# Tokens-on-partitions attention, a softmax minimum as bias, DMA turns, and gate products on GpSimd

## The chip, the cores and the metric

The kernel runs on one core of a Trainium2 chip. The metric is the device time of one execution in microseconds. Beside the times there is a profile of one execution: for every instruction its engine, start, duration, tiles and source line, and for every DMA its packets. PE is the tensor engine (its weight loads are shown as PEld), DVE the vector engine, ACT the scalar engine, POOL is GpSimd, SP the engine that issues most DMAs of this kernel.

## The reference

Linformer attention, then a gated feed-forward network. There are 8 batches and 8 heads, 1024 tokens and 64 columns a head; keys and values are projected from 1024 tokens to 64.

```python
k_proj = einsum('ks,bhsd->bhkd', E, k)
v_proj = einsum('ks,bhsd->bhkd', F, v)
scores = q @ k_proj^T / sqrt(64)
scores = scores - max(scores, axis=-1)
attn   = exp(scores) / (sum(exp(scores)) + 1e-9)
x      = (attn @ v_proj), heads side by side      # 8192 x 512
gate   = sigmoid(x @ w_gate)                      # 512 x 1536
val    = x @ w_val
out    = (gate * val) @ w_out                     # 8192 x 512, float32
```

## The kernel before

**Tiling.** Everything on PE is bf16 with float32 sums in eight PSUM banks (`pF0..3`, `pA0..3`). A batch is two blocks of 512 tokens; 1024 tokens of a head are held as 128 partitions x 8 rows, and two tokens' 64-column head rows share one 128-column piece (`g` = 0, 1 says which of the two). The feed-forward work of a block is done with Strassen-like seven-product schemes (`seven`, `o_jobs`): a product is four (or twelve) matmuls of 256 columns, ACT copies a bank to another bank or to SBUF in between (`copyG`, `snapG`, `copyO`, ...), DVE adds banks to SBUF buffers (`plus`). A *quad* K is one third of a block's gate and value work, so a batch has six quads and two output blocks. `quad_jobs` makes for a quad four gate tiles (`tanh` on ACT, since the sigmoid is taken as (1 + tanh(x/2))/2) and four gate products into `hT` (`hidden`, L1276). In two of the four, the value is still in PSUM; in the other two both gate and value lie in SBUF, in the spare buffers. `s_sum` forms sums of `hT` on DVE for the output products, and `xs_sum` forms sums of `xT` for the quads.

**Attention of a batch b >= 1.** POOL issues the loads of K, V and Q as one DMA each (`load_kv`, `load_q`), which turn float32 to bf16. `kv` projects K and V (L503 matmuls of 128x64 weights and 512 columns), `keep_kd` and `keep_vd` take the result out with ACT, `turn_kd` turns K by a DMA transpose on SP (L1526), and `transpose_q` turns Q in four (L1449). `sc_one` makes the scores with the 64 projected keys on partitions and tokens in the free dimension, four matmuls of 64x64 weights side by side; `h_exp` takes the exponential of a whole 128x512 bank in one ACT instruction, without the maximum. `den8` sums over keys with PE, `rec` takes reciprocals on DVE, `gather` (8 small DMAs) and `spread` (POOL `partition_broadcast`, L1618, into the K/V tiles) lay them out, `xo_one` multiplies by the values, and `mul` (L1649, DVE) scales the result into `xT`. In batch 1 the reciprocals are spread by PE matmuls and ACT copies instead (`out_jobs_pe`, with `bck`). Batch 0 has its own code (`h_*`).

**Order.** Each piece of work is a `job` on an engine with a position `pos`, counted in quads. `Scheduler.run` simulates the engines when the kernel is built, with costs given with every operation, and takes on each engine the ready job of lowest position, as long as it is within a `window` of PE's earliest open job and the banks and buffers that it needs are free. The order that comes out is the program of each engine; on the chip the engines run their lists strictly in order and wait on semaphores. `Plan.add` finds these waits from the keys that an operation reads (`r`), writes (`w`) or holds (`x`, the PSUM bank):

```python
            if o.eng == eng and o.dma is None:
                if eng == "PE":
                    return
            deps[id(o)] = o
```

So only PE is excused from waiting on its own engine. The same keys tie a bank's users together.

Of the kernel before, what the change touches and what calls it, by code (L numbers as in the profile page):

```python
# [6 lines left out]
AF = mybir.ActivationFunctionType  # L7
# [13 lines left out]
NI = DM // P  # L21

# [111 lines left out]
class Scheduler:  # L134
# [64 lines left out]
    def safe(self, group, got):  # L199
        left = {k: len(f) for k, f in self.free.items()}  # L200
        for g, _ in got:
            left[g.kind] -= 1
        taken = [g for g, _ in got]
        todo = []
        for g in self.groups + ([] if any(group is x for x in self.groups) else [group]):
            need, held = {"bank": 0, "buf": 0}, {"bank": 0, "buf": 0}
            for x in g:
                if x.at is None and not any(x is y for y in taken):
                    need[x.kind] += 1
                elif x.left:  # L210
                    held[x.kind] += 1
            todo.append((need, held))
# [11 lines left out]
    def take(self, j, t):  # L224
# [30 lines left out]
        return True  # L255

# [28 lines left out]
    def run(self):  # L285
# [17 lines left out]
        while left:  # L303
            moved = True
            while moved:
# [4 lines left out]
                for e in engines:  # L310
# [3 lines left out]
                    for item in sorted(self.open[e], key=lambda i: (i[0], i[1])):  # L314
                        if item[0] > limit:
                            break
# [17 lines left out]
def bass_linformer_attn__then__ffn_glu_sigmoid_kernel(  # L334
# [20 lines left out]
    with contextlib.ExitStack() as es:  # L355
# [9 lines left out]
        def within(shape, dtype):  # L365
# [21 lines left out]
        xS = [sbuf(f"xS{i}", [P, 4, 2, 256], BF16) for i in range(2)]  # L387
        early[0], used[0] = xS[0][:, :, :, :].rearrange("p a b c -> p (a b c)"), 0
# [3 lines left out]
        rhl = within([P, 256], BF16)  # L392
        quad = sbuf("quad", [P, 1], FP32)
# [12 lines left out]
        rb = (  # L406
            KVs[:, :, :, :].rearrange("p w h c -> p (w h c)").bitcast(FP32)
            .rearrange("p (n c) -> p n c", n=8)
        )
        rrow = (  # L410
            Qb[:, :, :].rearrange("p h c -> p (h c)").bitcast(FP32)
            .rearrange("p (i c) -> p i c", i=4)
        )
        kpd = sbuf("kpd", [64, H, 2, DH], BF16)
        kpD = sbuf("kpD", [P, H, DH], BF16)
        vpD = [sbuf(f"vpD{i}", [P, H, DH], BF16) for i in range(2)]
        qT = sbuf("qT", [P, H, 512], BF16)
        eT = sbuf("eT", [P, 8, 512], BF16)
        rden = sbuf("rden", [P, 256], FP32)
        xT = [sbuf(f"xT{i}", [P, NI, 2, 512], BF16) for i in range(2)]  # L420

# [6 lines left out]
        NB = 11  # L428
# [10 lines left out]
        sched = Scheduler(range(8), range(2 + NB), 20.6, 1.3, 38.8)  # L439
# [53 lines left out]
        def mm(b, o, lhsT, rhs, r, start=True, stop=True, tp=None, tr=False, read=False, n=512, conc=1, fill=0.0):  # L493
# [5 lines left out]
            else:  # L499
# [4 lines left out]
                r=r,  # L504
                x=[bk_(b)],
# [34 lines left out]
        def turned():  # L540
            return [("qT", r) for r in range(NR)]

        def load_kv(n, src, b, after=()):
            load(
                KV[n][:, :, :],
                src[b].rearrange("h (p t) d -> p h (t d)", t=NT),
                [("KV", n, 0), ("KV", n, 1)] + [("rb", 4 * n + x) for x in range(4)],
                f"KV{n}",
                r=list(after),
                nbytes=MB2,  # L550
            )
# [10 lines left out]
        def load_q(b):  # L562
            load(
                Qb[:, :, :],
                q[b].rearrange("h (p t) d -> p h (t d)", t=NT),
                [("Q", hf, R) for hf in range(2) for R in range(2)]
                + [("rrow", i, x) for i in range(4) for x in range(2)],
                "Q",
                nbytes=MB2,
            )  # L570
# [189 lines left out]
        def v_part(R):  # L760
# [14 lines left out]
            vv = vpD[0][:, :, :].rearrange("p (r h) d -> p r h d", h=2)  # L775
            for n, (h, g) in enumerate(((0, 0), (1, 1), (0, 1), (1, 0))):
                o = vv[64 * g : 64 * g + 64, pairs(R), h, :]
                i = bank[bks[h]][64 * h : 64 * h + 64, 0:128].rearrange("p (r d) -> p r d", d=DH)
                ws = [("vpD", 0, h, g, R)]
# [5 lines left out]
        def turn_k(R):  # L785
            bk = whole.next()
            ob = bank[bk][:, :].bitcast(BF16)
            for n, r in enumerate((2 * R, 2 * R + 1)):
# [11 lines left out]
                kpD[:, 4 * R : 4 * R + 4, :].rearrange("p h c -> p (h c)"),  # L800
                ob[:, 0:256],
                [],
                [("kpD", R)],
# [3 lines left out]
        def VPD(s, R):  # L807
            return [("vpD", s, h, g, R) for h in range(2) for g in range(2)]
# [28 lines left out]
        def h_sc(hf, R, bks):  # L837
            for rr in range(2):
                for c in range(2):
                    h = 4 * R + 2 * rr + c  # L840
                    for g in range(2):
# [4 lines left out]
                            kpD[gg, h, :],  # L846
                            qT[gg, h, 256 * hf : 256 * hf + 256],
                            [("kpD", R), ("qTh", hf, R, rr)],
# [9 lines left out]
        def h_den(Rs, bk):  # L858
            for n in [2 * R + g for R in Rs for g in range(2)]:
                for c in range(4):  # L860
# [5 lines left out]
                        [("dsel8", n % 2), ("eT", n)],  # L866
# [51 lines left out]
        def h_xo(R, bks):  # L918
            for rr in range(2):
                for g in range(2):  # L920
                    for c in range(2):
# [5 lines left out]
                            vpD[0][kk, h, :],  # L927
                            eT[kk, 2 * R + g, 256 * rr : 256 * rr + 256],
                            VPD(0, R) + [("eT", 2 * R + g)],
# [9 lines left out]
        def h_scale(hf, n, bk):  # L939
            R, g = n // 2, n % 2  # L940
            o = xT[0][:, 2 * R : 2 * R + 2, hf, 256 * g : 256 * g + 256]
# [12 lines left out]
        def h_scale_part(hf, n, j, bk):  # L954
# [4 lines left out]
                    xT[0][:, 2 * R + j, hf, 256 * g : 256 * g + 256],  # L959
# [119 lines left out]
        def mm_one(blk, m, i, n, pb):  # L1079
# [5 lines left out]
                xT[s][:, i, hf, :],  # L1085
                [("w" + n, m // 2, i // 2), ("xT", s, i, hf, 0), ("xT", s, i, hf, 1)],
# [45 lines left out]
        def x_part(blk, n):  # L1132
            s, hf = blk // 2 % 2, blk % 2
            if n[0] == "S":
# [3 lines left out]
                xT[s][:, i0 : i0 + 2, hf, 256 * tok : 256 * tok + 256],  # L1138
                [("xT", s, i0 + i, hf, tok) for i in range(2)],
            )  # L1140

        def xs_sum(blk, n):
# [7 lines left out]
            if blk == 2:  # L1150
                w = w + ["bsel8", ("kp", 0), ("kp", 1)]
                w += [(k, R) for k in ("rhi", "rhl") for R in range(2)]
# [99 lines left out]
        def quad_jobs(K, pos):  # L1252
# [4 lines left out]
            def gate(half_, tok, b, s, p):  # L1257
# [6 lines left out]
                job("ACT", p + 0.01, body, name="tanh")  # L1264

            def value(half_, tok, b, s, p):
# [4 lines left out]
                def body():  # L1271
# [3 lines left out]
                    dve(  # L1275
                        lambda e: e.scalar_tensor_tensor(  # L1276
                            o,
                            y.rearrange("p (j c) -> p j c", j=2),
                            1.0,
                            x.rearrange("p (j c) -> p j c", j=2),  # L1280
# [91 lines left out]
        def o_jobs(blk, pos, step, last=False):  # L1372
# [52 lines left out]
            for n in (1, 2, 3):  # L1425
                s_jobs(n, min(pos, ready + 0.1 * n))
# [431 lines left out]
```

## Time and profile before

| | us |
|---|---|
| three runs | 536.17, 536.48, 533.93 |
| median | 536.17 |
| the profiled execution, its own time | 535.25 |
| its span in the profile | 533.5 |

The span runs from the first to the last recorded instruction; the execution's own time has some microseconds around it. Per engine the page gives busy time, number of instructions and, for each group, the mean duration and the idle time before it with what ended it. The 40 slices cut the span into pieces of 13.3 us. Busy durations overlap at the ends where an engine starts one instruction before the one before has ended, so starts are also read from the timeline.

| group | count | mean ns |
|---|---|---|
| matmul, 128x128 weights, 256 columns, any product | most of 4757 | 273 |
| ACT 128x512 from PSUM to a spare buffer | 266 | 598 |
| DVE gate product, both inputs in SBUF (`hT<-spare`) | 76 | 736 |
| DVE gate product, value in PSUM | 36 and 33 | 675 and 678 |
| POOL `PARTITION_BROADCAST` | 96 | 892 |
| DMA transpose of Q, issue to landing | 24 | 3300 |

### The profile page before, as it was taken

What the parts mean: (1) busy time and instruction counts of PE and PEld (TensorE: products, weight loads), DVE (VectorE), ACT (ScalarE), POOL (GpSimd) and SP (SyncE); (2) the same over time, 40 slices, a digit from 0 to 9 for tenths busy, and PEclk for the clock granted to TensorE, in tenths of its full rate; (3) what the DMA queues carried; (4) which work ended last, traced back from release to release, by engine and by line L of the source; (5) the groups of instructions that cost most, each with busy time, mean ns of one, the idle gap of its engine ahead of it and who ended that gap; (6) DMA issues with size and microseconds to landing.
All of it is one profiled execution on the core that took longest, in us unless ns stands there. A gap on an engine that the chain in (4) does not pass through costs nothing.

```text
span 533.5 us, 11685 instructions
## 1 busy us (share of the span) xinstructions
PE 513.3 (96%) x4757; PEld 408.6 (77%) x4757; DVE 418.0 (78%) x730; ACT 362.5 (68%) x659; POOL 109.5 (21%) x148
## 2 busy tenths in 40 slices
PE   5899789999999999999999999999999999999995
PEld 4545557678887878778887888878787888888884
DVE  5569769759887698858987698967987798968683
ACT  2556766787677766876678766777668766676761
POOL 9400010109010801026010621008000440000000
PEclk9999989999999999999999999999999999999999
DMA  9999895972986178903884076901831020202022
GB/s 162 199 199 191 129 151 97 188 132 90 122 154 122 41 131 131 187 14 65 165 138 108 14 150 92 221 16 51 144 64 73 4 80 1 80 2 80 1 80 79
DMA packets 72949, 55.34 MB, mean 104 GB/s; under 512 B 31104, under 2 KB 64576, under 8 KB 72896
## 3 DMA queue, kind: packets, MB, share of 16 engines
q0 software_dynamic: 33984, 29.89, 37.3%
q1 hardware_dynamic: 38912, 24.72, 17.7%
q8 instruction: 37, 0.61, 0.4%
q14 instruction: 16, 0.13, 0.1%
HBM read 60.29 MB, written 16.78 MB: 144 GB/s over the span
## 4 chain that ended last, share of the span: by engine, by line
PE 90%; DMA 4%; DVE 3%; ACT 2%; POOL 1%; issue 0%; DVEq 0%; POOLq 0%
PE pF L503 46%; PE pA L503 44%; DMA KVs<-in_v_dram 2%; DMA kpD<-kpd 2%; ACT spare L516 1%; DVE wT L1308 1%; DVE spare L1208 1%; DVE hT L1276 0%; ACT eT L516 0%; POOL KVs L536 0%; POOL Qb L536 0%; ACT kpd L516 0%; DVE rden L877 0%; DVE rden L1594 0%; DVE ost L1405 0%
## 5 line engine op out<-in xcount | busy, mean ns | idle before, releaser
L1618 POOL PARTITION_BROADCAST KVs<-Qb x96 | 73.1, 892 | 168.4 <-PE pA L503 64.8
L516 ACT ACTIVATE spare<-pA 128x512 f32<-128x512 f32 x142 | 84.2, 598 | 21.8 <-PE pA L503 20.0
L516 ACT ACTIVATE spare<-pF 128x512 f32<-128x512 f32 x124 | 73.4, 598 | 22.0 <-PE pF L503 20.4
L1208 DVE TENSOR_TENSOR spare<-pF,spare 128x512 f32<-128x512 f32 x84 | 57.6, 686 | 32.5 <-ACT spare L516 20.6
L1208 DVE TENSOR_TENSOR spare<-pA,spare 128x512 f32<-128x512 f32 x81 | 55.5, 685 | 24.9 <-ACT spare L516 20.4
L516 ACT ACTIVATE spare<-spare 128x512 f32<-128x512 f32 x82 | 51.6, 630 | 15.2 <-DVE spare L1208 14.6
L1276 DVE SCALAR_TENSOR_TENSOR hT<-spare 128x512 bf16<-128x512 f32 x76 | 55.9, 736 | 0.5
L503 PE MATMUL pF<-wO,hT 128*128 128x256 bf16 x336 | 45.1, 273 | 1.4 <-DVE wT L1308 1.4
L503 PEld LDWEIGHTS pF<-wO,hT 128*128 128x128 bf16 x336 | 32.0, 98 | 7.3 <-DVE wT L1308 1.6
L503 PE MATMUL pA<-xT,wG 128*128 128x256 bf16 (+1 forms) x212 | 34.7, 285 | 0.1
L503 PE MATMUL pF<-xT,wV 128*128 128x256 bf16 (+1 forms) x204 | 33.6, 287 | 0.0
L503 PE MATMUL pA<-xT,wV 128*128 128x256 bf16 (+1 forms) x204 | 33.3, 285 | 0.0
L503 PE MATMUL pF<-xT,wG 128*128 128x256 bf16 (+1 forms) x196 | 32.2, 286 | 0.1
L503 PE MATMUL pA<-wO,hT 128*128 128x256 bf16 x240 | 32.2, 273 | 0.0
L536 POOL DMA_DIRECT2D KVs<-in_k_dram x9 | 8.0, 884 | 117.4 <-PE pA L503 44.0
L516 ACT ACTIVATE pF<-pA 128x512 f32<-128x512 f32 x36 | 21.4, 593 | 15.6 <-PE pA L503 12.0
L503 PE MATMUL pA<-xS,tG 128*128 128x256 bf16 x208 | 31.2, 273 | 0.3 <-ACT spare L516 0.3
L503 PE MATMUL pF<-xS,wG 128*128 128x256 bf16 x208 | 31.1, 273 | 0.0
L503 PE MATMUL pA<-xS,wV 128*128 128x256 bf16 x200 | 30.0, 273 | 0.0
L503 PE MATMUL pF<-wT,hS 128*128 128x256 bf16 x216 | 28.5, 273 | 0.0
L516 ACT ACTIVATE pA<-pF 128x512 f32<-128x512 f32 x30 | 17.6, 586 | 15.9 <-PE pF L503 13.6
L503 PE MATMUL pF<-xS,tV 128*128 128x256 bf16 x184 | 27.6, 273 | 0.2 <-ACT spare L516 0.2
(164 smaller groups left out, 1158.8 us busy)
## 6 DMA issues: line engine op xcount, KB each, us to landing
out_dram<-ost SPq DMA_DIRECT2D x64, 256.0 KB, 2.5
KVs<-in_k_dram POOLq DMA_DIRECT2D x7, 1024.0 KB, 9.2
KVs<-in_v_dram POOLq DMA_DIRECT2D x7, 1024.0 KB, 17.2
Qb<-in_q_dram POOLq DMA_DIRECT2D x7, 1024.0 KB, 11.7
wO<-in_moe_w_out_dram POOLq DMA_DIRECT2D x1, 1536.0 KB, 12.7
wG<-in_moe_w_gate_dram POOLq DMA_DIRECT2D x5, 256.0 KB, 18.8
wV<-in_moe_w_val_dram POOLq DMA_DIRECT2D x5, 256.0 KB, 19.4
KVs<-in_k_dram POOLq DMA_DIRECT2D x2, 512.0 KB, 9.0
```

Of the source, the lines that this page charges most:

```text
L503: lambda e: e.matmul(o, lhsT, rhs, **kw),
L516: lambda e: e.activation(o, i, func, scale=scale),
L536: add("POOL", lambda e: e.dma_start(o, i), r=r, w=w, dma=sem, cost=0.88, nbytes=nbytes)
L1208: lambda e: e.tensor_tensor(BF(s), PB(b)[:, :], BF(s), ALU.add),
L1276: lambda e: e.scalar_tensor_tensor(o, y.rearrange("p (j c) -> p j c", j=2), 1.0, x.rearrange("p (j c) -> p j c", j=2), ALU.add, ALU.mult,),
L1308: dve(lambda e: e.tensor_tensor(T[n], a, b, op), r, w, n=1536, rate=1.92)
L1618: lambda e: e.partition_broadcast(rb[0:parts, n, :], rrow[32 * j : 32 * j + 1, i, :], channels=parts),
```

## The change

- For b >= 1 the scores have tokens on partitions: `score` uses a turned Q piece as weights and a K tile `kpD` that holds the two tokens' keys as blocks on a diagonal, with -1/8 in it. `lowest` takes the minimum of each 64 keys on DVE (the negated scores' minimum is the maximum). `exps` then takes, for each 64 columns, one ACT exponential with that minimum as a per-partition bias.
- `turn_p` turns the exponentials by DMA. `outs` multiplies by a value tile `vpD` with a column of ones, so that the sums come with the product; `divide` takes the reciprocal and scales on DVE; `turn_x` turns the result into `xT` by DMA. The exponentials (`pt`) and the results (`xt`) lie in the K and V tiles.
- `den8`, `rec`, `gather`, `spread`, `out_jobs_pe` and the loading of a POOL library go.
- In `quad_jobs`, where value and gate both lie in SBUF, POOL adds one to the gate and makes the product; DVE keeps the two with the value in PSUM.
- Loads are split in two by heads, and those of a batch wait until the four `xTt` of the batch before have landed. Two spare buffers are dropped (11 to 9). The layout of `xT` changes, and batch 0's tiles move.
- Positions come from a table `AT`; the scheduler lets jobs of a group that is already running pass the window, and counts clean banks in `safe`.

```diff
+AT = dict(
+    window=1.49, step=0.106, lag=0.432, ostep=0.511, tanh=1.634, hidden=0.056, oa=0.63, ob=3.387,
+    sums=0.483, late=0.626, sc=0.69, scs=0.246, out=1.569, outs=0.299, loads=6.109, gap=0.071,
+    kv=6.048, tq=7.187, xa=6.048, xb=2.71, w0=2.548, ws=0.597, kv1=3.347, qt1=4.589, sc1=4.172,
+    scs1=0.063, late1=-2.498, out1=4.151, outs1=0.014, osum=0.345, loads2=5.971, tq2=6.24,
+    kv2=5.751, xa2=6.757, xb2=9.188, o0=4.699, o0s=0.01, xs1=3.544, sc2=1.894, end=0.137,
+)
...
+        pt, xt = [KVs[:, i, :, :].rearrange("p h c -> p (h c)").rearrange("p (t c) -> p t c", t=4) for i in range(2)]
+        kpd = sbuf("kpd", [P, H, P], BF16)
+        kpD = sbuf("kpD", [P, H, P], BF16)
+        vpD = [sbuf(f"vpD{i}", [P, H, 2, DH + 1], BF16) for i in range(2)]
...
-        NB = 11
+        NB = 9
...
-                job("ACT", p + 0.01, body, name="tanh")
+                job("ACT", p + AT["tanh"], body, name="tanh")
+                if b is None:
+                    job(
+                        "POOL",
+                        p + AT["tanh"] + 0.01,
+                        lambda: pool(
+                            lambda e: e.tensor_scalar(BF(g), BF(g), 1.0, None, op0=ALU.add),
+                            [bf_(g)],
+                            [bf_(g)],
+                            cost=0.8,
+                            port=True,
+                        ),
+                        name="one",
+                    )
...
+                    if b is not None:
+                        dve(
+                            lambda e: e.scalar_tensor_tensor(o, yy, 1.0, xx, ALU.add, ALU.mult),
+                            [bf_(g)],
+                            w,
+                            b=b,
+                        )
+                    else:
+                        pool(
+                            lambda e: e.tensor_tensor(o, xx, yy, ALU.mult),
+                            [bf_(g), bf_(s)],
+                            w,
+                            cost=1.2,
+                            port=True,
+                        )
...
+        def score(t, y, bk):
+            for x in range(4):
+                h = 4 * y + x
+                mm(
+                    bk,
+                    PB(bk)[:, x * P : (x + 1) * P],
+                    qT[:, h, t * P : (t + 1) * P],
+                    kpD[:, h, :],
+                    ["kpD", ("qT", h // 2)],
...
+        def lowest(t, y, bk):
+            n = 16 * t + 8 * y
             dve(
+                lambda e: e.tensor_reduce(
+                    low[:, n : n + 8],
+                    PB(bk)[:, :].rearrange("p (n k) -> p n k", n=8),
+                    mybir.AxisListType.X,
+                    ALU.min,
+                ),
...
+        def exps(t, y, bk, xs):
+            for x in xs:
+                n = 16 * t + 8 * y + x
+                c = 512 * y + 64 * x
+                add(
+                    "ACT",
+                    lambda e, x=x, n=n, c=c: e.activation(
+                        pt[:, t, c : c + 64],
+                        PB(bk)[:, 64 * x : 64 * x + 64],
+                        AF.Exp,
+                        bias=low[:, n : n + 1],
+                        scale=-1.0,
+                    ),
+                    r=[("low", t, y), "projected"],
+                    w=[("pt", t, y, x)],
+                    x=[bk_(bk)],
+                    cost=0.12,
+                )
+
+        def turn_p(t):
...
+                lambda e: e.dma_start_transpose(eT[:, :, t * P : (t + 1) * P], pt[:, t, :]),
+                r=[("pt", t, y, x) for y in range(2) for x in range(8)] + kv_keys(0),
...
+        OUTS = ((0, 3), (3, 6), (6, 8))
+
+        def outs(b, t, hh, bk):
+            for h in range(*hh):
+                c = 130 * (h - hh[0])
+                mm(
+                    bk,
+                    PB(bk)[:, c : c + 130],
+                    eT[:, h, t * P : (t + 1) * P],
+                    vpD[b % 2][:, h, :, :].rearrange("p g d -> p (g d)"),
...
+        def divide(t, hh, bk):
...
+                lambda e: e.reciprocal(i, o[:, :, DH]),
...
+                lambda e: e.tensor_tensor(
+                    xt[:, t, :].rearrange("p (g h d) -> p h g d", g=2, h=H)[:, hh[0] : hh[1], :, :],
...
+        def turn_x(b, t):
...
+                lambda e: e.dma_start_transpose(
+                    xT[s][:, hf, :, :, c : c + P].rearrange("p g i c -> p (g i) c"), xt[:, t, :]
...
+        def score_jobs(b, pos, step, late):
+            for t in range(4):
+                for y in range(2):
+                    new_group()
+                    bk = new_bank()
+                    p = pos + step * (2 * t + y)
+                    job("PE", p, lambda t=t, y=y, bk=bk: score(t, y, bk), name="sc")
+                    job("DVE", p + late, lambda t=t, y=y, bk=bk: lowest(t, y, bk), name="low")
+                    for xs in ((0, 1, 2, 3), (4, 5, 6, 7)):
+                        job("ACT", p + late, lambda t=t, y=y, bk=bk, xs=xs: exps(t, y, bk, xs), name="exp")
+                job("SP", pos + step * (2 * t + 1), lambda t=t: turn_p(t), name="turnp")
...
             if p + 1 < B:
-                score_jobs(p + 1, base + 0.3, 0.2)
+                score_jobs(p + 1, base + AT["sc2" if p == 1 else "sc"], AT["scs"], AT["late"])
+                out_jobs(p + 1, base + AT["out"] + (AT["sc2"] - AT["sc"]) * (p == 1), AT["outs"], AT["late"])
                 if p + 2 < B:
-                    kv_jobs(p + 2, base + 1.5)
-                spread_jobs(base + 1.6)
-                if p + 2 < B:
-                    job("POOL", base + 3.0, lambda p=p: load_q(p + 2), name="loadq")
-                    turn_q(base + 4.2)
-                out_jobs(p + 1, base + 2.8, 0.45)
-                if p + 3 < B:
-                    loads_kv(p + 3, base + 4.6, turned())
-                x_sums(2 * p + 2, base + 4.9)
+                    loads(p + 2, base + AT["loads"], landed_x((p + 1) % 2))
+                    turn_q(base + AT["tq"])
+                    kv_jobs(p + 2, base + AT["kv"])
+                x_sums(2 * p + 2, base + AT["xa"])
```

## The prediction

> **What bounds the kernel now.** I read the page first: busy time by engine, then the 40 slices.
>
> ```profile
> PE 513.3 (96%) x4757; PEld 408.6 (77%) x4757; DVE 418.0 (78%) x730; ACT 362.5 (68%) x659; POOL 109.5 (21%) x148
> ...
> PE   5899789999999999999999999999999999999995
> ...
> PEclk9999989999999999999999999999999999999999
> ```
>
> TensorE is busy nearly everywhere, with the granted clock below nine tenths in one slice only. The table by stretches makes it exact (busy us and instructions of PE, PEld, DVE, ACT, POOL, then clock, DMA share, GB/s):
>
> ```profile
> 60.00:80.00 20.00, 15.33 (x140) 9.99 (x139) 12.04 (x19) 13.58 (x26) 2.64 (x3) 0.91 1.03 160
> 100.00:160.00 60.00, 60.00 (x557) 48.43 (x554) 49.10 (x83) 44.26 (x81) 17.56 (x21) 1.00 0.72 129
> ```
>
> From 100 us to 460 us PE is hardly idle (59.3 to 60.0 of every 60), and one batch takes about 61 us of it; DVE has some 11 us to spare in 60, ACT 15.7 us. So work taken from DVE or POOL earns nothing there; only PE work does, and anything that makes PE wait costs its full length. What attention costs PE today is in the PE timeline (start, duration, op):
>
> ```profile
> 104.73 0.60 PE L503 MATMUL pF<-xT,tV 128*128 128x256 bf16 x4
> 105.26 0.40 PE L503 MATMUL pA<-qT,kpD 64*64 64x512 bf16 x1
> ...
> 105.61 0.61 PE L503 MATMUL pF<-xS,tG 128*128 128x256 bf16 x4
> ...
> 110.76 0.62 PE L503 MATMUL pA<-eT,dsel 128*32 128x256 bf16 x16
> 111.31 0.61 PE L503 MATMUL pA<-xS,wV 128*128 128x256 bf16 x4
> ```
>
> Products of four start 0.44 us apart, so a group of four score matmuls takes 105.61 - 104.73 - 0.44 = 0.44 us with its lead-in, four groups 1.76. The denominators take 0.55 + 0.09 = 0.64. The value products (124.51 to 124.85 the same way) take 0.43 x 4 = 1.72. Sum 4.1 us per batch.
>
> **PE part of the change.** Per batch it issues 32 + 32 matmuls with 128x128 weights and 128 or 130 columns. The nearest row is the PE transposes of Q: eight of 128 columns from 58.35 to 58.80, 0.056 us each. 64 x 0.056 = 3.6 us, 0.5 less than 4.1; seven batches: -3.5. Batch 1 also loses its 16 matmuls that spread reciprocals (`pA<-xS 32*128`, four from 82.27 to 82.59; four groups near 0.4): -1.6. Together **-5.1 us**.
>
> **ACT part, where I expect the loss.** `h_exp` did a batch in 8 instructions of 128x512. The softmax minimum is a per-row bias, one for each head half, so `exps` issues 64 of 128x64. All eight of a bank name `bk_(bk)` in `x`, and `Plan.add` excuses only PE from waits on its own engine; each exp waits for the end of the one before. The trace has that pattern in the two `keep_vd` halves, beside the unchained exps (ACT timeline):
>
> ```profile
> 106.41 0.63 ACT L516 ACTIVATE eT<-pF 128x512 bf16<-128x512 f32 x1
> 106.89 1.12 ACT L516 ACTIVATE eT<-pA 128x512 bf16<-128x512 f32 x2
> ...
> 118.70 1.02 ACT L516 ACTIVATE kpd<-pF 64x1024 bf16<-64x1024 f32 x1 [0.83 <-PE pF L503]
> 119.62 0.58 ACT L516 ACTIVATE spare<-pA 128x512 f32<-128x512 f32 x1
> 120.23 1.22 ACT L516 ACTIVATE vpD<-pF 64x512 bf16<-64x512 f32 x2
> ```
>
> Unchained, starts are 0.48 us apart although each lasts 0.60. Chained, two of 0.59 last 1.22 end to end: no overlap, and about 0.03 us between. For the length of a 64-column exp: 128x512 takes 0.597, 128x128 (`xS<-pA`) 0.278, so 0.83 ns a column and 0.225 for 64; with the gap **0.255 us**. Bounds: 0.12, the issue price that the planner gives it in the diff (if the chain cost nothing), and 0.31, the spacing of the chained 64x128 halves. 64 x 0.255 = 16.3 us a batch against 8 x 0.48 = 3.8: +12.5 us of ACT. The halves of `kd` (2 x 0.6 for 1.02) add 0.2.
>
> The trace has no bias from a tile. The Trainium skill (ScalarE: Activation LUTs, What ACT_TABLE_LOAD costs) says that such a pointer operand adds about 93 ns to an ACTIVATE; by that, as an estimate, an exp would be 0.35 us and a batch 22 us, and the stall below would be 6 us larger in each batch. No row here shows it, and the sum leaves it out.
>
> Does 12.5 fit into 15.7 us of idle in 60? Only if spread over the period. The instruction order is fixed when the kernel is built, with an exp at 0.12 us: 7.7 us for a batch. While the exps run, ACT falls 16.3 - 7.7 = 8.6 us behind its order. Queued behind them on ACT are the copies and snapshots of the three chains (`copyG`, `snapV`, ...), each of which frees or fills a PSUM bank for the next product but one: PE, in order too, waits and does not get the time back, being full. Some lag is absorbed: at 103.5 to 111.4 ACT ran without a gap; eight exps put 3.8 us into 4.8 us in which the other evictions would have needed 0.57 x 4.8 = 2.7 (70 evictions x 0.494 us in 61), 1.7 us over, and PE showed no idle. So 8.6 - 1.7 = **6.9 us a batch** (between 0 and 15, see the rivals). Six steady batches: +41. Batch 1 falls where ACT had 6.4 us idle in 20 and loses its 8 copies `bck` (3.9 us): 12.5 - 3.9 - 6.4 = 2.2; with two DMA turns newly in that chain I take +3 (0 to 7).
>
> **Parts that I cost at nothing.** *DVE*, per batch period: out go 12 SBUF gate products x 0.736 = 8.8, 8 multiplies x 0.68 = 5.5 and 2 reciprocals x 0.95 = 1.9; in come 8 minima (128x512 from PSUM, 0.685: 5.5), 12 divisions of 384 or 256 columns (between the rows 0.415 and 0.681: 6.1) and 12 short reciprocals (0.17 as the shortest DVE rows, at most 0.95: 2 to 11). Net -2.6 to +7 on 49 of 60 us: covered. If the cover were gone, PE would wait for `plus` and `hT`. *POOL* loses 16 broadcasts x 0.89 = 14 us and gets 12 adds and 12 products; no POOL elementwise row exists, so from the DVE row, 0.74 to 1.5 each: 18 to 36 us, plus six load issues x 0.88 = 5.3; at most 41 of 61 us. But POOL now feeds `hT`, and its loads wait for `xTt`; products queue behind them, and `sum1..4` and `O` products wait for those. The planner holds an output block until later, so I take 0 (up to 3 a batch). A rule against this move is in the Trainium skill (GPSIMD Engine Reference, Elementwise): a two-input op costs POOL about 2.6 cycles an element, about twice DVE; by its 4497 ns for 2048 columns, 1.1 us for ours, an estimate, inside my bounds. *SP* issues 13 turns (1.35 each, 17.6 us) instead of 4 + 1 turns and 8 gathers (5.5 + 1.2 + 4.4): +6.5 us on a queue that mostly waits for `ost`. *PSUM and spare buffers*: two buffers fewer, 0 to 1 a batch, taken as 0.
>
> **Sum** against the profiled execution (535.25 us, span 533.5): 535.25 - 5.1 + 41 + 3 = 574. The median of the three runs is 0.9 above it: **575 us**.
>
> **Rivals.**
> *Hidden (faster).* The lag vanishes, because the exps are placed where ACT idles or cost 0.12. For: 12.5 is under 15.7, and the 103.5 burst cost PE nothing. Against: eight exps are 2.0 us a bank and banks follow each other at 0.246 of a quad (2.5 us) with 1.4 us of other evictions. It decides if a bank's exps take under 1.1 us. Time: 535.25 - 5.1 + 0.9 = 531.
> *Half hidden.* Deferred `tanh` (now 1.634 quads later in rank) give way and half of the 6.9 is recovered: 6 x 3.5 + 3 - 5.1 + 536.2 = 555.
> *The ring of loads binds.* `pt` and `xt` lie in the K/V tiles, so a batch's loads start only when the last xT has landed. Ring: loads 37.3% of 533.5 = 199 us for 29.89 MB, 21 us for a batch's 3.15; Q turns 5.5 + 2.0; exps and first minimum 17.3; turn of p 3.3; products and division 1.5; turn of x 3.3: 54 us, inside 61. If the exps get only the ACT time that the other evictions leave (43%), they take 38 us and the ring 76: +15 a batch, 6 x 15 + 3 - 5.1 + 536.2 = 624. For: in-order ACT mixes them. Against: overdue exps rank first.
> *The moves change nothing* because PE stays full and its 5.1 us are lost again to small waits: 536.
>
> **How the numbers follow.** Main case 0.42, hidden 0.18, ring 0.18, half hidden 0.16, nothing 0.06. Of this kernel a measurement can tell about 0.5% (2.7 us) from no change. Faster is the hidden case, 0.18; same 0.06; slower the rest, 0.76. The range reaches from 528, 3 us below the hidden case (if part of the 4.7 us that PE idles from 60 to 80 us is filled too), to 622, leaving less than a tenth at each end.
>
> **What would show it.** ACT: 448 exps of 128x64 with starts about 0.25 us apart (0.12 or 0.35 would each change the sum). PE idle of about 7 us in each batch, ended by ACT (`spare`, `pA`, `pF` evictions), in the stretch where the exps run, ACT there near 100%. Matmuls of 128 columns at 0.056 us. DVE under 75%, no PE idle ended by it. Wrong if PE idle after 100 us stays under 10 us in all, if it is ended by DMA (ring) or POOL, or if exps are spread evenly.

## The result and the profile after

The changed kernel takes **633.66 us** (median of four runs, 629.7 to 638.44) beside 535.44 for the kernel before (four runs): a ratio of 1.184, interval 1.174 to 1.194. The forecast was 575 us with a range up to 622: the right side, but 12 us beyond the range. The profiled execution took 631.39 us with a span of 629.6, so it stands 96.1 us above the one of before in time and in span alike.

The page after, first part (busy time by engine) and the slices:

```profile
PE 540.7 (86%) x4853; PEld 430.2 (68%) x4853; DVE 433.2 (69%) x796; ACT 455.0 (72%) x1050; POOL 306.0 (49%) x256
...
PE   5999579986989699977989789986898868999996
...
PEclk9999869988999899988999899998999999999999
```

Two things are read here. PE was idle 629.6 - 540.7 = 88.9 us, before 533.5 - 513.3 = 20.2: **+68.7 us of idle**. And its busy time grew by **27.4 us**. The two make the 96.1. The clock row shows where part of the second comes from: it is below nine tenths in nine slices where before it was in one, and its mean is 0.966 (before 0.997). The table by stretches (PE, PEld, DVE, ACT, POOL, clock, DMA share, GB/s), where before had 59.3 to 60.0 us of PE in every 60:

```profile
100.00:160.00 60.00, 50.96 (x432) 40.27 (x430) 39.06 (x71) 46.84 (x117) 29.30 (x24) 0.91 0.73 139
280.00:340.00 60.00, 53.82 (x472) 43.86 (x471) 43.81 (x82) 45.95 (x105) 34.22 (x27) 0.95 0.69 128
400.00:460.00 60.00, 49.97 (x445) 38.97 (x443) 40.30 (x75) 47.78 (x119) 24.65 (x19) 0.97 0.59 112
```

ACT is busy 46 to 48 of 60 here; it isn't full over the minute, it is full in the stretch that matters. What it does there (ACT timeline), and PE beside it:

```profile
132.58 1.34 ACT L1640 ACTIVATE KVs<-pA,low 128x64 bf16<-128x64 f32 x4
133.82 0.59 ACT L531 ACTIVATE pF<-pF 128x512 f32<-128x512 f32 x1
134.34 1.34 ACT L1640 ACTIVATE KVs<-pA,low 128x64 bf16<-128x64 f32 x4
135.57 0.59 ACT L531 ACTIVATE ost<-pF 128x512 f32<-128x512 f32 x1
```

```profile
132.42 0.61 PE L517 MATMUL pA<-kpD,qT 128*128 128x128 bf16 x8
134.47 0.61 PE L517 MATMUL pF<-xT,wG 128*128 128x256 bf16 x4 [1.43 <-ACT pF L531]
135.73 0.40 PE L517 MATMUL pA<-kpD,qT 128*128 128x128 bf16 x4 [0.66 <-ACT KVs L1640]
135.97 0.97 PE L517 MATMUL pF<-xS,tG 128*128 128x256 bf16 x4
```

Within a bank the exps start 0.346 us apart (the median over the trace; eight in a row take 2.74 us), so 64 of them are 22.1 us a batch. The copy `pF<-pF` is due behind four of them, and PE stands 1.43 us until it has ended. The groups of ACT (count, busy us, mean ns, idle before) give the length of one, 313 ns:

```profile
L1640 ACT ACTIVATE KVs<-pF,low 128x64 bf16<-128x64 f32 x232 | 71.5, 313 | 7.3 <-DVE low L1623 1.4
L1640 ACT ACTIVATE KVs<-pA,low 128x64 bf16<-128x64 f32 x216 | 66.3, 313 | 8.1 <-DVE low L1623 2.8
```

PE's waits (total us, times, longest) were led by ACT, the exps first; ACT ended 60 of the 82 us of waits that the view lists. Before, the longest total that ACT ended was 2.1 us:

```profile
PE pA L517 <- ACT KVs L1640: 12.1, 14, 2.2
PE pF L517 <- ACT KVs L1640: 11.4, 15, 2.4
PE pA L517 <- ACT pA L531: 10.1, 8, 3.7
PE pF L517 <- ACT spare L531: 9.4, 11, 1.6
PE pA L517 <- ACT spare L531: 6.0, 9, 1.3
```

And the chain that ended last has 26% of ACT in it, most of it exps (by line):

```profile
PE pF L517 28%; PE pA L517 26%; ACT KVs L1640 17%; ACT spare L531 4%; DMA KVs<-in_v_dram 4%; DVE hS L1354 2%; DVE spare L1220 2%; ACT EF L531 1%; DMA kpD<-kpd 1%; ACT pA L531 1%; DVE KVs L1694 1%; POOL hT L1311 1%; ACT kpd L531 1%; ACT ost L531 1%; ACT pF L531 1%
```

So the mechanism of the forecast is there. The questions for the experiments: is it the exps alone, and what in them (the tile bias, the waits of ACT on itself, or their number); does the order or the ring of loads add; and what does the GpSimd half of the change cost.

### The profile page after: what moved, and what is told of

It is laid out like the page before. It is cut to its first block, busy times and chain, and to the rows that moved or that the text cites. A ratio compares the mean times of both kernels' runs of the same rounds, so it can differ in the third digit from the quotient of the medians.

```text
span 629.6 us, 12700 instructions
## 1 busy us (share of the span) xinstructions
PE 540.7 (86%) x4853; PEld 430.2 (68%) x4853; DVE 433.2 (69%) x796; ACT 455.0 (72%) x1050; POOL 306.0 (49%) x256
## 4 chain that ended last, share of the span: by engine, by line
PE 54%; ACT 26%; DVE 7%; DMA 6%; issue 4%; POOL 2%; SPq 0%; DVEq 0%; ACTq 0%; POOLq 0%
PE pF L517 28%; PE pA L517 26%; ACT KVs L1640 17%; ACT spare L531 4%; DMA KVs<-in_v_dram 4%; DVE hS L1354 2%; DVE spare L1220 2%; ACT EF L531 1%; DMA kpD<-kpd 1%; ACT pA L531 1%; DVE KVs L1694 1%; POOL hT L1311 1%; ACT kpd L531 1%; ACT ost L531 1%; ACT pF L531 1%
## 5 line engine op out<-in xcount | busy, mean ns | idle before, releaser
L1282 POOL TENSOR_SCALAR spare<-spare 128x512 f32<-128x512 f32 x73 | 111.2, 1525 | 169.9 <-ACT spare L531 141.5
L531 ACT ACTIVATE spare<-pF 128x512 f32<-128x512 f32 x131 | 77.2, 595 | 33.9 <-PE pF L517 32.9
L531 ACT ACTIVATE spare<-pA 128x512 f32<-128x512 f32 x124 | 73.3, 596 | 33.5 <-PE pA L517 32.5
L1311 POOL TENSOR_TENSOR hT<-spare 128x512 bf16<-128x512 f32 x55 | 72.2, 1315 | 40.8 <-DVE spare L1220 19.3
L1640 ACT ACTIVATE KVs<-pF,low 128x64 bf16<-128x64 f32 x232 | 71.5, 313 | 7.3 <-DVE low L1623 1.4
L1640 ACT ACTIVATE KVs<-pA,low 128x64 bf16<-128x64 f32 x216 | 66.3, 313 | 8.1 <-DVE low L1623 2.8
L1282 POOL TENSOR_SCALAR EF<-EF 128x512 f32<-128x512 f32 x17 | 26.4, 1551 | 53.8 <-ACT EF L531 37.4
L1354 DVE TENSOR_TENSOR hS<-hT 128x1024 bf16<-128x1024 bf16 (+1 forms) x32 | 28.2, 882 | 14.9 <-POOL hT L1311 14.2
L1304 DVE SCALAR_TENSOR_TENSOR hT<-spare,pA 128x512 bf16<-128x512 f32 x37 | 25.2, 682 | 17.5 <-PE pA L517 13.6
L517 PE MATMUL pA<-xS,wG 128*128 128x256 bf16 x192 | 28.9, 273 | 6.2 <-ACT KVs L1640 2.0
L517 PEld LDWEIGHTS pA<-wO,hT 128*128 128x128 bf16 x288 | 27.8, 99 | 6.1 <-issue 2.2
```

The lines of the kernel that those rows point to most:

```text
L517: lambda e: e.matmul(o, lhsT, rhs, **kw),
L531: lambda e: e.activation(o, i, func, scale=scale),
L1282: lambda e: e.tensor_scalar(BF(g), BF(g), 1.0, None, op0=ALU.add),
L1304: lambda e: e.scalar_tensor_tensor(o, yy, 1.0, xx, ALU.add, ALU.mult),
L1311: lambda e: e.tensor_tensor(o, xx, yy, ALU.mult),
L1354: lambda e: e.tensor_tensor(o, a, b, op),
```

## The experiments

All numbers side by side. The time is the median of two to nine runs, the ratio is to the kernel before as it ran beside each, and the last three columns are of one profiled execution. "PE idle" is the span less PE's busy time on the page; "exp" is the work of one bank of scores on ACT.

| kernel | exp | time, us | ratio to before, interval | PE busy | PE idle | clock |
|---|---|---|---|---|---|---|
| before | 1 x 512 | 535.44 | | 513.3 | 20.2 | 0.997 |
| changed | 8 x 64, bias | 633.66 | 1.184, 1.174 to 1.194 | 540.7 | 88.9 | 0.966 |
| e1_unchained | 8 x 64, bias | 586.68 | 1.096, 1.080 to 1.112 | 529.9 | 58.3 | 0.983 |
| e7_const_bias | 8 x 64 | 592.32 | 1.105, 1.097 to 1.114 | 527.7 | 61.3 | 0.989 |
| e2_wide | 2 x 256 | 552.83 | 1.033, 1.027 to 1.039 | 518.4 | 32.9 | 0.992 |
| e9_ring_longer | 2 x 256 | 565.56 | 1.057, 1.051 to 1.063 | 522.1 | 39.6 | 0.987 |
| e8_wide_short_add | 2 x 256 | 548.95 | 1.025, 1.007 to 1.042 | 517.9 | 25.3 | 0.993 |
| e3_gates_dve | 8 x 64, bias | 641.62 | 1.199, 1.186 to 1.212 | 546.1 | 91.3 | 0.958 |
| e4_wide_gates_dve | 2 x 256 | 555.96 | 1.039, 1.028 to 1.050 | 521.4 | 34.9 | 0.991 |
| e5_before_gates_pool | 1 x 512 | 726.23 | 1.355, 1.349 to 1.361 | 544.4 | 180.4 | 0.879 |
| e6_measured_costs | 8 x 64, bias | 641.17 | 1.197, 1.182 to 1.211 | 550.6 | 85.7 | 0.925 |
| e10_bank_max_dve | 1 x 512, bias | 537.13 | 1.0056, 1.0029 to 1.0083 | 514.5 | 19.9 | 1.000 |
| e11_bank_max_pool | 1 x 512, bias | 542.07 | 1.013, 1.009 to 1.018 | 516.0 | 25.2 | 0.995 |
| e12_bank_max_loads | 1 x 512, bias | 546.27 | 1.020, 1.018 to 1.022 | 516.7 | 27.3 | 0.987 |

**What in an exp costs.** First the waits of ACT on itself. The exps name their bank as read, not as held, so that none waits for the one before; the order of every engine stays that of the changed kernel.

```diff
-                    r=[("low", t, y), "projected"],
+                    r=[("low", t, y), "projected"] + ([] if sched.now is not None else [bk_(bk)]),
                     w=[("pt", t, y, x)],
-                    x=[bk_(bk)],
+                    x=[bk_(bk)] if sched.now is not None else [],
```

> Changed kernel with every order kept; the eight exps of a bank hold it as readers, so none waits for the end of the one before. Theory A (ACT falls behind its order because the chained exps take 0.347 us each where the order allows 0.12): spacing falls to about 0.25 us, 64 x 0.1 = 6.2 us of ACT less a batch, time 633 to about 590-600. Theory B (GpSimd's gate products and the DVE slowed beside them carry the loss): within 5 us of 633. Theory C (the ring of loads, turns and exps binds, DMA part): within 10 us of 633.

The ACT timeline of that kernel, over the same banks:

```profile
130.66 0.98 ACT L1640 ACTIVATE KVs<-pA,low 128x64 bf16<-128x64 f32 x4
131.44 0.68 ACT L531 ACTIVATE pF<-pF 128x512 f32<-128x512 f32 x1
131.96 1.00 ACT L1640 ACTIVATE KVs<-pA,low 128x64 bf16<-128x64 f32 x4
```

Four exps and the step to the copy take 131.44 - 130.66 = 0.78 us, 0.196 each, less than the 0.25 that was expected, and the time falls by 47 us. So of the 0.346 us between starts, 0.15 were only the chain. The tile bias by itself, with the chain kept (the maximum is then not subtracted):

```diff
                         AF.Exp,
-                        bias=low[:, n : n + 1],
                         scale=-1.0,
```

> Changed kernel with every order and every wait kept; the 64 exps of a batch have no bias from a tile (the maximum is not subtracted). If the tile bias is what makes an exp 0.313 us long instead of the 0.225 that I had predicted: spacing 0.347 to 0.25, time about as with the unchained exps, 585-600. If the length comes from elsewhere: 625-640.

```profile
L1640 ACT ACTIVATE KVs<-pF 128x64 bf16<-128x64 f32 x232 | 50.9, 224 | 7.1 <-DVE low L1623 1.4
L1640 ACT ACTIVATE KVs<-pA 128x64 bf16<-128x64 f32 x216 | 47.2, 224 | 7.3 <-DVE low L1623 2.1
```

The exp lasts 224 ns and starts are 0.256 us apart: the 0.225 and 0.255 of the forecast. The bias adds 89 ns to an instruction, and over the kernel 41 us of time. Removed one at a time, chain and bias give 47 and 41 us of the 98; no run took both away with 64 columns kept, so the two can't be added. The bias isn't hidden where the chain is absent: where an exp follows one of another bank, and so waits for none, the starts are 0.212 us apart in the changed kernel and 0.121 in e7_const_bias, the same 0.09 us. Then the number of instructions: two of 256 columns a bank, no bias, everything in the same order (again without the maximum).

```diff
+            if sched.now is None:
+                c, n = 512 * y + 64 * xs[0], 64 * len(xs)
+                add("ACT", lambda e: e.activation(
+                        pt[:, t, c : c + n], PB(bk)[:, 64 * xs[0] : 64 * xs[0] + n], AF.Exp, scale=-1.0),
+                    r=[("low", t, y), "projected"], w=[("pt", t, y, x) for x in xs], x=[bk_(bk)])
+                return
```

> Changed kernel with every order kept; two exps of 128x256 a bank without a bias in place of eight of 128x64 with one (the maximum is not subtracted; DVE still takes it). ACT time of a batch's exps falls from 22 us to 16 x 0.41 = 6.5 us, less than the 7.7 us that the order allows. A: most of the loss goes, 545-565. B: 600 or more. C: 590-620, since loads and turns stay as they are.

552.83 us: **81 of the 98 us** go with the exps, by length and number. PE idle falls from 88.9 to 32.9 us. What stays, 17 us above before, has other causes: by the profiles 12.7 us more PE idle, and 5.1 us more of PE's busy time (518.4 beside 513.3).

**The order.** The planner had an exp at 0.12 us and the addition on GpSimd at 0.8. With the measured costs it makes another order from the same table of positions:

```diff
-                            cost=0.8,
+                            cost=1.4,
...
-                    cost=0.12,
+                    cost=0.347,
```

> Changed kernel with nothing but the planner's costs corrected to the profile (an exp 0.347 us instead of 0.12, the add on GpSimd 1.4 instead of 0.8), positions kept, so another fixed order. Theory O (the loss is the wrong order: an order that knows the true length spreads the exps over ACT's idle time): below 590. A with ACT short of time where the exps must run (between the turned Q and the next loads): 610-640.

641.17 us, no better than the changed kernel (intervals 1.182 to 1.211 and 1.174 to 1.194 overlap). At these positions, a planner that knows the price doesn't find a place for the exps, so "planned too cheap" alone isn't what costs. Whether positions searched anew with the measured costs would have spread narrow exps over ACT's idle time wasn't run. PE idle is 85.7 us there, and the clock lower still.

**GpSimd.** The gate additions and products put back on DVE, alone and with the wide exps:

```diff
-                job("POOL" if b is None else "DVE", p + AT["hidden"], body, name="hidden")
+                job("DVE", p + AT["hidden"], body, name="hidden")
```

(the product's body and the addition as in the kernel before; e4_wide_gates_dve has the edit of e2_wide as well).

> Changed kernel with the gate products of two SBUF inputs back on DVE as one instruction and the add on GpSimd gone; the order is planned anew. A: exps stay, 600-630. B: 550-570. C: 620-635.

> Both edits: wide exps without a bias (the maximum is not subtracted) and gate products on DVE. A with B as the rest: what is left is the new layout with its DMA turns and 5 us less PE work, 527-540. C: above 560, with PE idle ended by DMA.

Neither gains, and both lie outside what was expected of them: 641.62 beside 633.66, 555.96 beside 552.83, with overlapping intervals in both pairs. But these orders are new ones for a table of positions made with the gates on GpSimd, so they bound the move only loosely. The other side of it, the move alone in the kernel before, whose GpSimd also broadcasts the reciprocals (broadcasts and gate work made to wait for each other):

```diff
+                job("POOL", p + 0.02, ...)   # adds one to the gate, as in the changed kernel
...
-                job("DVE", p + 0.01, body, name="hidden")
+                job("POOL" if b is None else "DVE", p + 0.01, body, name="hidden")
...
-                w=[("rb", n), ("KV", n // 4, n % 4 // 2)],
+                w=[("rb", n), ("KV", n // 4, n % 4 // 2)] + turns(),
```

> Kernel before with only the GpSimd part: the gate products of two SBUF inputs and the add of one move to GpSimd, planned anew; broadcasts and products on GpSimd wait for each other. A (the move by itself is not what costs): 536-545. B (GpSimd at 1.5 us an add and the DVE sums slowed beside it are a large part of the loss): above 555.

726.23 us, the worst of all. The POOL timeline over one batch's broadcasts says why:

```profile
211.97 5.24 POOL L1638 PARTITION_BROADCAST KVs<-Qb  x6 [5.88 <-issue]
...
232.33 1.52 POOL L1273 TENSOR_SCALAR spare<-spare 128x512 f32<-128x512 f32 x1 [7.83 <-issue]
```

GpSimd stands 5.9 to 7.8 us at each change between the two kinds of instruction, whatever the profile names as releaser: 24 changes, 158 us in all, beside 160 us more of PE idle than before. So this run says little about the changed kernel, which has no broadcasts: the move needs them gone, which the token layout does. How long GpSimd's own part is, from e2_wide, with only the addition cut to one column (one is then added to that column only):

```diff
-                            lambda e: e.tensor_scalar(BF(g), BF(g), 1.0, None, op0=ALU.add),
+                            lambda e: e.tensor_scalar(BF(g)[:, 0:1], BF(g)[:, 0:1], 1.0, None, op0=ALU.add),
```

> The kernel with wide exps (553 us) with every order and wait kept, but GpSimd's add of one covers one column instead of 512 (so one is added to that column alone, and the maximum is not subtracted). If GpSimd's add, 1.49 us where the order allows 0.8, carries what is left of the loss: 536-543. If DVE, DMA or the order carry it: 548-554.

548.95 beside 552.83; the intervals 1.007 to 1.042 and 1.027 to 1.039 don't separate them. The two runs lie 7.6 us apart, and the profile, of the faster one, has 7.6 us less of PE idle. The median lies in the range expected if something else carries what is left. The addition is then worth some 4 us by the medians and 8 by the profiles, an estimate, of the remaining 17.

**The ring of loads.** From e2_wide, the last `xT` turn of each batch is issued twice; the second waits for the first, and the loads for both. The second lands 3.1 us after the first in five of the six batches whose next loads wait for it, and 4.9 us after it in one. The edit:

```diff
+            if sched.now is None and t == 3:
+                add("SP",
+                    lambda e: e.dma_start_transpose(
+                        xT[s][:, hf, :, :, c : c + P].rearrange("p g i c -> p (g i) c"), xt[:, t, :]),
...
+                    w=[("xTt", s, t)], dma=f"xT{t}")
```

> The kernel with wide exps (553 us) with every order kept; the last DMA turn of each batch's x is done twice, the second after the first has landed, so the ring from one batch's loads to the next is about 3.3 us longer in each of the six steady batches. C (that ring sets the steady pace of what is left): 568-576. Not C: 551-557.

565.56 us, between the two ranges expected: +12.7 us for some 20 put in. With short exps the ring is close to setting the pace, and about two thirds of a lengthening reach the time. In the changed kernel the same ring was longer: on SP's queue the last `xT` turns of two batches end near 309.4 and 385.3, 75.9 us apart, and between them the turns of the exponentials are strung out by the exps:

```profile
352.35 13.43 SPq L1656 DMA_TRANSPOSE eT<-KVs  x3
365.95 3.22 SPq L1710 DMA_TRANSPOSE xT<-KVs  x2
374.96 1.27 SPq L1656 DMA_TRANSPOSE eT<-KVs  x1
378.23 7.09 SPq L1710 DMA_TRANSPOSE xT<-KVs  x2
```

**A version made from this.** A softmax is unchanged by what is subtracted, as long as it is the same for all keys of a row and no row's exponentials overflow or all vanish. A common maximum can't make them overflow; a row far below the others of its bank could vanish. So one minimum over the whole bank (the two tokens and four heads of a partition) serves eight rows, and one exp of 128x512 takes it as its bias: 56 exps, not 448. With the positions searched again for it, gates on DVE (e10, with the edit of e3_gates_dve) or on GpSimd (e11):

```diff
-                    low[:, n : n + 8],
-                    PB(bk)[:, :].rearrange("p (n k) -> p n k", n=8),
+                    low[:, n : n + 1],
+                    PB(bk)[:, :],
...
-                        pt[:, t, c : c + 64],
-                        PB(bk)[:, 64 * x : 64 * x + 64],
+                        pt[:, t, c : c + 512],
+                        PB(bk)[:, :],
```

> New version on the layout of the changed kernel: one minimum for a whole bank row (512 columns instead of 64, the softmax is unchanged by it), so one exp of 128x512 a bank with a tile bias; gate products on DVE; positions searched again with these costs (an exp 0.6 us). A: with ACT's exps at 8 x 0.6 = 4.8 us a batch nothing of the large loss is left: 533-545; it beats the kernel before only if the layout's PE work is smaller, which the traces of the other runs speak against.

> The same with the gate products on GpSimd (add 1.4 us in the plan), positions searched for it. A: 535-550. B (GpSimd and the sums beside it cost even in an order made for them): above 555.

537.13 and 542.07 us. Page and groups of e10_bank_max_dve:

```profile
PE 514.5 (96%) x4853; PEld 426.2 (80%) x4853; DVE 448.4 (84%) x886; ACT 361.8 (68%) x658; POOL 51.9 (10%) x76
...
PEclk9999999999999999999999999999999999999999
...
L1612 ACT ACTIVATE KVs<-pA,low 128x512 bf16<-128x512 f32 x31 | 21.0, 690 | 7.9 <-DVE low L1597 7.7
L1612 ACT ACTIVATE KVs<-pF,low 128x512 bf16<-128x512 f32 x25 | 17.2, 688 | 8.1 <-DVE low L1597 8.0
```

The whole loss is gone with the maximum, the DMA turns and the token layout all in place; it is 0.6% slower than before, which these runs can just tell. Exps, gates and positions changed together here, so the step from 553 to 537 isn't split between them. The gates on GpSimd cost 5 us more here, each with its own search, so order and engine aren't apart in that difference. Some of e10's last idle ended on loads of V, so a last search, with e10's kernel, took slower DMA into account:

```diff
-            self.pipe = begin + j.bytes / 390e3
+            self.pipe = begin + j.bytes / 290e3
...
-    window=1.31, step=0.105, lag=0.252, ostep=0.483, tanh=25.07, hidden=0.105,
+    window=8.558, step=0.099, lag=0.179, ostep=0.581, tanh=29.195, hidden=3.072,
```

> One minimum for a row over a whole bank and one 128x512 exponential per bank, gate products on DVE, as in e10_bank_max_dve, but the table of positions is searched again with a planner in which the loads of K and V and the DMA turns are slower (290 GB/s in place of 390), since the PE idle that was left in e10_bank_max_dve ended mostly on the loads of V (4.6 of 7.7 us after 100 us). Theory that the order around the loads is what is left: PE idle ended by KVs loads falls below 1.5 us and the time to 532 to 535. Rival, that e10_bank_max_dve is already at what PE allows (PE busy 514.5 us, 96% of the span, as in the kernel before): 535.5 to 539, with PE busy at 513 to 516 and idle of the span at 19 to 22 us.

546.27, a miss for both theories. The steady part did improve, and batch 1 was spoilt: PE's stretches in e12_bank_max_loads (columns as above)

```profile
40.00:100.00 60.00, 47.24 (x411) 35.24 (x410) 49.83 (x102) 32.27 (x58) 1.62 (x2) 0.89 0.67 109
100.00:160.00 60.00, 59.36 (x563) 50.34 (x561) 50.38 (x101) 42.66 (x79) 7.79 (x12) 1.00 0.88 151
280.00:340.00 60.00, 59.47 (x566) 50.85 (x564) 51.38 (x100) 43.96 (x79) 4.45 (x6) 1.00 0.77 141
```

against 58.58, 59.79 and 58.13 us of PE in e10. From 100 to 460 us e12 has 357.2 us of PE, e10 353.1; from 40 to 100 it has 11.3 less, and waits there 5.7 us for a division and 5.1 for the turn of K:

```profile
PE pA L513 <- DVE KVs L1667: 7.2, 4, 5.7
...
PE pF L513 <- DMA kpD<-kpd: 5.1, 1, 5.1
```

A table with e10's batch 1 and e12's steady part should come to about 537.1 - 4.1 = 533, an estimate, level with before; it wasn't run. No version beat the kernel before.

## Why the prediction failed, step by step

**The ACT part: right place, wrong size.** The step that failed is "the length of a 64-column exp": 0.225 with the gap 0.255 us, "bounds 0.12 ... and 0.31". Measured were 313 ns and 0.346. The trace of before had no tile bias, and the sum left it out. The sentence that drew on the Trainium skill (ScalarE: Activation LUTs, What ACT_TABLE_LOAD costs: about 93 ns for a pointer operand, an exp at 0.35 us, 22 us a batch, 6 us more stall in each batch) was right about the exp: 313 - 224 = 89 ns at 64 columns, 690 - 598 = 92 at 512 (against a copy of that size), 0.346 us, 22.1 us a batch. Its stall was a little high: from e7_const_bias to the changed kernel PE idle grows by 27.6 us, 4.6 in each of six batches. With it the same sum gives 574 + 6 x 6 = 610, and the upper bound of an exp would have been 0.35.

e7_const_bias is the kernel that the sum was made for, exps at 0.255: it took 592, not 575. Its PE idle is 61.3 - 20.2 = 41.1 us above before, where the sum had 41 + 3 = 44. That looks like a hit, but is partly luck: 12.7 of the 41.1 are still there with short exps (e2_wide), so the exps make 28.4, about 4 us in each of seven batches and not 6.9; ACT seems to have taken up more lag than the 1.7 us I allowed. At 0.346 they make 88.9 - 32.9 = 56 us, 8 a batch. Idle isn't proportional to the spacing: 0.196, 0.256 and 0.346 us gave 58, 61 and 89 us. The 17 us by which e7_const_bias misses the sum are in PE's busy time, 527.7 - 513.3 = +14.4 us where -5.1 was forecast; the next two parts take this up.

**The clock, which the sum held fixed.** This is the second failed step. PE's busy time for the same 4853 matmuls is 514.5 us in e10 at clock 1.000 and 540.7 in the changed kernel at 0.966: 26 us that come on top of idle. The mean clock hides what happens. In the changed kernel's trace the granted clock after 40 us is 1.00 or 0.50 and nothing between; around the first wait shown above it goes like this:

| stretch, us | PE busy, us | matmuls | clock |
|---|---|---|---|
| 132.7 to 136.1 | 1.31 | 16 | 0.99 |
| 136.1 to 139.5 | 3.40 | 21 | 0.50 |
| 139.5 to 153.1 | 8.39 | 72 | 1.00 |

Eight stretches of 3.4 to 13.7 us are at 0.50, 41 us together (before: one of 3.4), and in the 3.4 us ahead of each PE was busy only 1.30 to 1.53 us. PE was busy 32.8 us in the eight, so the clock explains at most half of that, 16 of the 26 us (an estimate). Much of the rest may be the breaks themselves: PE's busy time falls into 124 unbroken pieces here and 31 in e10, and at each break a last matmul of 0.27 us counts in full where the next would have started 0.11 us after it: 93 x 0.16 = 15 us at most, an estimate. It seems to matter how close together the waits fall, not only how much idle they make: e6_measured_costs, with 86 us of idle, has 96 us at 0.50, and e1_unchained, with 58, has 17. Neither this nor that the waits cause the slow stretches was tried by itself.

**The PE part.** "Together -5.1 us" isn't there: at the full clock PE is 1.2 us busier than before (514.5 against 513.3). The single prices held: in e2_wide four score matmuls step on after 0.22 us, three of 130 columns after 0.19. But with their lead-ins the new products take 28.4 us in e2_wide, where 64 x 0.056 in seven batches is 25.1, and before's groups had been charged from a lead-in each: adding up their pieces of PE's time after 40 us, without idle, the scores, denominators, values and spreading took 27.0 us (28.7 plus 1.6 in the forecast). The projections of K and V grew from 12.9 to 14.9.

**The parts costed at nothing.** DVE: the minima took 0.687 us, the reciprocals 0.19, the divisions 0.56 and 0.42, all inside the bounds, and DVE's share was 69%, under the 75% named (of a span 18% longer than before's). "No PE idle ended by it" failed: DVE ended about 11 us of it after 100 us. POOL: the addition took 1.525 us, just over the bound of 1.5, the product 1.3; the estimate from the Trainium skill (GPSIMD Engine Reference, Elementwise) was 1.1. Groups of the changed kernel:

```profile
L1282 POOL TENSOR_SCALAR spare<-spare 128x512 f32<-128x512 f32 x73 | 111.2, 1525 | 169.9 <-ACT spare L531 141.5
L1311 POOL TENSOR_TENSOR hT<-spare 128x512 bf16<-128x512 f32 x55 | 72.2, 1315 | 40.8 <-DVE spare L1220 19.3
...
L1354 DVE TENSOR_TENSOR hS<-hT 128x1024 bf16<-128x1024 bf16 (+1 forms) x32 | 28.2, 882 | 14.9 <-POOL hT L1311 14.2
```

So DVE's sums waited 14.2 us for GpSimd's products, as the text warned, and e8 puts the addition at up to 8 us: within "up to 3 a batch", not the 0 that was taken.

**The rivals.** *Hidden* (531) and *half hidden* (555) assumed exps that fit in; they didn't. *The ring* (624) was the nearest number. Its condition, exps that get only ACT's leftover time, was met in part: a batch's exps stretched over up to 35 us (38 in the rival), and the ends of its `xT` turns on SP's queue came 67 to 76 us after those of the batch before (76). In the changed kernel ring and PE's in-order waits both grow from the same exps, and no run took the ring away there, so their shares stay open; e9 shows most of a longer ring in the time once the exps are short. As I read it, the main case and this rival were one story told twice, and a range that stopped at 622 cut off what the two give together. With 0.18 on a case at 624, that range didn't leave "less than a tenth" above it either. "Wrong if it is ended by DMA or POOL" didn't come true: ACT ended most of the idle, 60 of 82 us of waits.

## What to carry to other kernels

Count what one instruction becomes before what it computes: eight exponentials of 64 columns with a bias of their own cost ACT 2.8 us where one of 512 costs 0.69, so look for a bias that serves the whole tile. Look at which engines wait on their own last instruction; that alone was 0.15 of 0.346 us. And when TensorE is full, price its idle with what goes with it: here 69 us more of idle came with 27 us more of PE's busy time, of which a clock at one half in short stretches is at most 16.

## What the runs showed of the chip that I had not expected

- An ACT instruction that waits for its own engine's last one starts 0.03 us after that has ended (0.346 us between starts at 313 ns, 0.256 at 224). Without that wait the same exps started 0.196 us apart, well before the last one's end (each is then recorded as 0.51 to 0.56 us long, e1_unchained).
- GpSimd's addition of a constant, one input, float32 in place, took 1.525 us for 128x512; its product of two inputs took 1.315.
- GpSimd stood 5.9 to 7.8 us at each of 24 changes between `PARTITION_BROADCAST` and elementwise work (e5_before_gates_pool).
- The granted clock of TensorE went from 1.00 to 0.50 for 3.4 us and more after 3.4 us in which PE was busy 1.30 to 1.53 us, though after 100 us no single gap in PE's work was over 2.8 us (changed kernel).
- With elementwise work on GpSimd, DVE's sums of two SBUF tiles got longer: 128x512 `hS<-hT` from 413 to 788 ns, 128x1024 from 684 to 977. Without it, in e3_gates_dve, they took 417 and 683; in e11_bank_max_pool, with it in another order, 415 and 1032, so not every sum is hit. Groups of before and of the changed kernel:

```profile
L1323 DVE TENSOR_TENSOR hS<-hT 128x512 bf16<-128x512 bf16 x16 | 6.6, 413 | 0.0
```

```profile
L1354 DVE TENSOR_TENSOR hS<-hT 128x512 bf16<-128x512 bf16 x16 | 12.6, 788 | 5.3 <-POOL hT L1311 5.3
```
